# A selection matrix 192 instead of 64 bytes wide: everything allocated behind it starts 128 bytes later

## The chip, the cores and the metric

The kernel runs on one core of a Trainium2 chip. The metric is the device time of one execution in microseconds (us), median of several runs. TensorE does the matmuls (PE in the rows, its weight loads PEld), VectorE is DVE, ScalarE ACT, GpSimd POOL, and the queue of SyncE (SP) issues most DMAs. On-chip memory has 128 partitions; an address here is an offset in bytes within a partition, the same in all of them.

## What is computed

Three stages, one behind the other (cut to what matters):

```
# 1: attention with keys and values pooled by 8   (4 x 8 heads, 576 x 64)
attn = softmax(scale * q @ k_p.T);  x = attn @ v_p          # -> x: 2304 x 512
# 2: a dense layer
h = x @ w_in;  x = (h * np.cos(h)) @ w_out                  # 512 -> 2048 -> 512
# 3: eight experts, all applied, weighted by P
P = exp(x @ w_gate - max), then 8 rounds of row and column normalization
for e in range(8):
    h = np.maximum(x @ w1[e], 0.0)                          # 512 -> 1024
    out += P[:, e:e+1] * (h @ w2[e])                        # 1024 -> 512
```

## The kernel before

Every float32 product is made of three single-pass matmuls on pieces: each operand is cut into a high part and a low rest (xh and xl, whi and wlo, gh and gl, vhi and vlo), and hi·hi, hi·lo and lo·hi are added in PSUM.

The program is written as a graph of nodes, each for one engine (`Graph.add`, L169); `Graph.schedule` puts them in one fixed order per engine by estimated times and due times, and a table of numbers (`SHIFTS`) corrects some of them. None of these estimates reads an address.

Stage 2 works on blocks of 384 tokens. `hidden1` (L894 to L896) multiplies weights wc with xh and xl, `cosine` makes gh and gl, and `output1` (the same three lines, tile po) multiplies weights wc with gh and gl as the **moving** operand, 384 columns. For its last two blocks it uses seven products in place of eight (`first_layer`, L1077) with sums xP of the tokens and differences dhi and dlo of the weights; half of the resulting pieces lie in tiles named gw.

Stage 3 takes pairs of blocks (3) and half experts (16 units). In `first_layer` (L1077) the weights whi and wlo are the stationary operand and xc, the tokens' pieces, the moving one, 384 columns: 2 × 7 × 6 = 84 matmuls a step. Its results become the pieces gh and gl (`strassen_result`, `g_split`, `halves`). In `strassen_layer` (L1457) these are the **stationary** operand, in slices of 128 columns (512 bytes), and the weights vhi and vlo the moving one, 256 columns: 3 × 42 = 126 matmuls a step. The 48 steps follow each other, with blocks of the next step's first layer between those of the second layer (`STRASSEN`). `accumulate` (L1444) adds a result to the output.

```
for n, (l, m) in enumerate(((gh, w[name][0]), (gh, w[name][1]), (gl, w[name][0]))):
    nc.tensor.matmul(out=ps, lhsT=l[:, r], rhs=m[:, k], start=(start and h + n == 0),
```

Memory is a stack from the left and one from the right. From the left, in the order of allocation, come the group `base` (the x tiles, the first-layer weights, four accumulators, and then wgr, sel and lg of the gate), the group `first` (raw, gph and gpl: gh and gl), and `second`, which is later replaced by `more` (two more accumulators, further tiles for gh and gl). `sel` is a small matrix for picking columns; line L1206 reads its first 8 columns. From the right come the groups early, mid, ahead and late, with vhi and vlo, s, c and sf.

Where tiles start in the built program, in bytes past a multiple of 512:

| tiles | before | after |
|---|---|---|
| xc, xh and xl of blocks 0 to 3, xP, gw, spare; whi, wlo, wc in `base` | 192 | 192 |
| gh, gl; raw, wsum, xd; r; wc in `second`; xh and xl of blocks 4 and 5; two accumulators | 320 | 448 |
| vhi, vlo; dhi, dlo (some dhi, dlo: 448); sf, s, c | 128 | 128 |

Of the kernel before, what the change touches and what calls it, by code (L numbers as in the profile page):

```python
# [23 lines left out]
P = 128  # L24
T = B * S
DM = H * D
KC = DM // P
FU = 512
FC = FU // P
E = 8  # L30
# [3 lines left out]
NT = T // P  # L34
# [6 lines left out]
GW = 32  # L41
# [102 lines left out]
class Graph:  # L144
# [18 lines left out]
    def buf(self, kind, shape, dtype, name):  # L163
        return Buf(kind, shape, dtype, name)
# [268 lines left out]
def fused_kernel(ctx: ExitStack, tc: tile.TileContext, qT, kT, vT, v0, k1, v1, wa1, wb1, wa2, wb2, wg, out):  # L433
# [731 lines left out]
    for u in range(U1):  # L1165
# [16 lines left out]


    gate = {n: buf(k_gc[n], s, F32, n) for n, s in (
        ("ones", [P, P]), ("wgr", [P, KC, GW]), ("sel", [P, 2 * E]), ("lg", [P, NT, E]), ("pr", [P, NT, E]))}
    ones, wgr, sel, lg, pr = (gate[n] for n in ("ones", "wgr", "sel", "lg", "pr"))
    add("V", 0.17, lambda: nc.vector.memset(ones.tile, 1.0), [], [ones])
    load(lambda: wgr.tile, lambda: wg, P * KC * GW * 4, writes=[wgr])
# [397 lines left out]
```

## Time and profile before

| | |
|---|---|
| median of 3 runs | 1930.12 us (1927.75 to 1932.39) |
| the profiled execution | 1929.34 us, its span 1927.6 us |
| TensorE busy, matmuls / weight loads | 1907.3 / 1872.0 us, 13012 of each |
| VectorE, ScalarE, GpSimd busy | 1531.9, 1096.6, 427.4 us |
| mean granted TensorE clock | 0.999 of full speed |
| moved by DMA | 406.79 MB, 211 GB/s |

The span runs from the first to the last instruction; what lies around it is 1.7 us. A matmul's duration reaches from its start to the modelled end of its pipeline, so that successive matmuls overlap; the distance between two starts in the timeline says how fast they follow.

### The profile page before, as it was taken

The page shows a single profiled execution, that of the slowest core. Times are in us where ns is not written, and L with a number is a line of the kernel's source. Part 1 is how long each engine was busy: PE and PEld are TensorE (multiplying, and loading weights), DVE is VectorE, ACT ScalarE, POOL GpSimd, SP SyncE. Part 2 cuts the span into 40 slices and gives each one's busy share as a digit, 9 for nine tenths or more (in the row PEclk, how much of TensorE's full clock was granted, in tenths as well). Part 3 has the DMA queues.
Part 4 walks back from the last instruction along what each step waited for, and adds up shares of the span by engine and source line. Part 5 has one row for each costly group of instructions (what it writes and reads, how often), then busy time and mean ns, then how long its engine had stood idle before and what let it go on. Part 6 is the DMA issues. An engine that isn't in the chain of part 4 may idle for free.

```text
span 1927.6 us, 34292 instructions
## 1 busy us (share of the span) xinstructions
PE 1907.3 (99%) x13012; PEld 1872.0 (97%) x13012; DVE 1531.9 (79%) x2823; ACT 1096.6 (57%) x2354; POOL 427.4 (22%) x341
## 2 busy tenths in 40 slices
PE   8999999999999999999999999999999999999999
PEld 6789998899999999999999999999999999999998
DVE  8998888987787777777787787777777877877776
ACT  5664445675556666555556565565555565655553
POOL 2523245453202021212112021212121120212120
PEclk9999999999999999999999999999999999999999
DMA  8567564487656546546546455465465464554552
GB/s 294 169 193 236 194 198 138 176 288 239 231 225 229 228 186 237 212 181 236 211 177 262 168 231 229 184 238 210 183 236 211 178 262 170 229 231 180 229 216 113
DMA packets 107478, 406.79 MB, mean 211 GB/s; under 512 B 11825, under 2 KB 16561, under 8 KB 107313
## 3 DMA queue, kind: packets, MB, share of 16 engines
q1 hardware_dynamic: 106768, 403.55, 56.4%
q8 instruction: 102, 1.67, 0.4%
q0 software_dynamic: 544, 1.05, 0.3%
q14 instruction: 64, 0.52, 0.1%
HBM read 363.40 MB, written 41.16 MB: 210 GB/s over the span
## 4 chain that ended last, share of the span: by engine, by line
PE 91%; DVE 5%; ACT 1%; DMA 1%; issue 1%; POOL 0%; SPq 0%; DVEq 0%; POOLq 0%; ACTq 0%
PE pc L1457 21%; PE py L1077 17%; PE qc L1457 16%; PE pv L1077 11%; PE px L1077 11%; PE po L894 3%; PE po L895 3%; PE po L896 3%; PE ph L894 1%; PE ph L896 1%; PE ph L895 1%; PE ptr L803 0%; DVE at L540 0%; DVE cw L858 0%; PE psc L714 0%
## 5 line engine op out<-in xcount | busy, mean ns | idle before, releaser
L1457 PE MATMUL pc<-vhi,gl 128*128 128x256 f32 x1152 | 321.6, 279 | 0.0
L1457 PE MATMUL pc<-vhi,gh 128*128 128x256 f32 x1152 | 321.5, 279 | 0.0
L1457 PE MATMUL pc<-vlo,gh 128*128 128x256 f32 x1152 | 321.3, 279 | 0.0
L1077 PE MATMUL py<-xc,whi 128*128 128x384 f32 x1152 | 293.3, 335 | 0.0
L540 POOL TENSOR_TENSOR raw<-raw 128x512 f32<-128x512 f32 x45 | 59.1, 1314 | 895.4 <-DVE wlo L540 542.1
L540 DVE TENSOR_TENSOR gl<-sf,gh 128x384 fp32r<-128x384 f32 x384 | 228.4, 624 | 30.9 <-ACT gh L523 30.9
L523 ACT ACTIVATE gh<-sf 128x384 fp32r<-128x384 f32 x384 | 195.0, 524 | 92.1 <-DVE sf L540 90.1
L1457 PE MATMUL qc<-vhi,gh 128*128 128x256 f32 x864 | 243.6, 282 | 0.9 <-DVE qc L540 0.5
L1457 PE MATMUL qc<-vhi,gl 128*128 128x256 f32 x864 | 241.6, 280 | 0.0
L1457 PE MATMUL qc<-vlo,gh 128*128 128x256 f32 x864 | 240.8, 279 | 0.0
L1457 PEld LDWEIGHTS pc<-vlo,gh 128*128 128x128 f32 x1152 | 216.6, 188 | 0.0
L1457 PEld LDWEIGHTS pc<-vhi,gl 128*128 128x128 f32 x1152 | 216.3, 188 | 0.0
L1457 PEld LDWEIGHTS pc<-vhi,gh 128*128 128x128 f32 x1152 | 215.5, 187 | 0.1
L1077 PEld LDWEIGHTS py<-xc,whi 128*128 128x128 f32 x1152 | 199.7, 188 | 1.3 <-ACT py L523 0.6
L1077 PE MATMUL px<-xc,whi 128*128 128x384 f32 x768 | 195.8, 335 | 0.0
L1077 PE MATMUL pv<-xc,whi 128*128 128x384 f32 x768 | 195.8, 335 | 0.0
L1077 PE MATMUL py<-xc,wlo 128*128 128x384 f32 x576 | 193.2, 335 | 0.0
L1457 PEld LDWEIGHTS qc<-vhi,gh 128*128 128x128 f32 x864 | 161.8, 187 | 3.4 <-DVE qc L540 1.1
L1457 PEld LDWEIGHTS qc<-vlo,gh 128*128 128x128 f32 x864 | 162.5, 188 | 0.0
L1457 PEld LDWEIGHTS qc<-vhi,gl 128*128 128x128 f32 x864 | 162.3, 188 | 0.0
L1077 PEld LDWEIGHTS pv<-xc,whi 128*128 128x128 f32 x768 | 130.7, 188 | 0.0
L1077 PEld LDWEIGHTS px<-xc,whi 128*128 128x128 f32 x768 | 130.5, 188 | 0.0
(235 smaller groups left out, 4676.1 us busy)
## 6 DMA issues: line engine op xcount, KB each, us to landing
xc<-xc SPq DMA_DIRECT2D x357, 768.0 KB, 6.7
wc<-wac SPq DMA_DIRECT2D x112, 256.0 KB, 3.3
raw<-wa SPq DMA_DIRECT2D x48, 512.0 KB, 4.0
raw<-wb SPq DMA_DIRECT2D x48, 512.0 KB, 7.4
wac<-wc SPq DMA_DIRECT2D x64, 256.0 KB, 3.8
out<-acc SPq DMA_DIRECT2D x18, 256.0 KB, 2.0
qc<-qt SPq DMA_DIRECT2D x30, 128.0 KB, 3.1
wf<-cw SPq DMA_DIRECT2D x12, 256.0 KB, 3.6
```

What stands on the lines that cost most here:

```text
L523: lambda: nc.scalar.activation(out=out(), in_=in_(), func=func, **{k: v() if callable(v) else v for k, v in more.items()}),
L540: (nc.gpsimd if e == "G" else nc.vector).tensor_tensor(out=out(), in0=in0(), in1=in1(), op=op)
L894: nc.tensor.matmul(out=ps, lhsT=lh, rhs=rh, start=(i == 0), stop=False)
L895: nc.tensor.matmul(out=ps, lhsT=lh, rhs=rl, start=False, stop=False)
L896: nc.tensor.matmul(out=ps, lhsT=ll, rhs=rh, start=False, stop=(i == total - 1))
L1077: nc.tensor.matmul(out=ps(), lhsT=l[:, k], rhs=r[:, c, :], start=(start and c + n == 0), stop=(c + n == 3), skip_group_check=True)
L1457: nc.tensor.matmul(out=ps, lhsT=l[:, r], rhs=m[:, k], start=(start and h + n == 0), stop=(h + n == 3), skip_group_check=True)
```

## The change

The tile sel gets 48 columns of 4 bytes in place of 16. Only its first 8 are written and read, as before. The tiles behind it in the left stack start 128 bytes later; the instructions and their order are the same on all five engines.

```diff
     gate = {n: buf(k_gc[n], s, F32, n) for n, s in (
-        ("ones", [P, P]), ("wgr", [P, KC, GW]), ("sel", [P, 2 * E]), ("lg", [P, NT, E]), ("pr", [P, NT, E]))}
+        ("ones", [P, P]), ("wgr", [P, KC, GW]), ("sel", [P, 6 * E]), ("lg", [P, NT, E]), ("pr", [P, NT, E]))}
```

## Rows read from the trace of the kernel before

**Rows 1.** The page, part 1: busy us (share of the span) and instructions.
```profile
PE 1907.3 (99%) x13012; PEld 1872.0 (97%) x13012; DVE 1531.9 (79%) x2823; ACT 1096.6 (57%) x2354; POOL 427.4 (22%) x341
```
**Rows 2.** Chain of waits from 600 us to the end, shares by line.
```profile
by line: PE pc L1457 28.9%; PE qc L1457 21.8%; PE py L1077 21.0%; PE pv L1077 14.0%; PE px L1077 14.0%; DVE acc L1444 0.1%; issue 0.1%; DVE qc L540 0.0%
```
**Rows 3.** Windows view of 600 to 1900 us: busy us (instructions) by engine.
```profile
core 0: us, PE busy (x) PEld busy (x) DVE busy (x) ACT busy (x) POOL busy (x), PEclk, DMA share, GB/s
600.00:1900.00 1300.00, 1300.00 (x9272) 1298.31 (x9271) 1004.53 (x1832) 737.09 (x1634) 217.90 (x159) 1.00 0.55 212
```
**Rows 4.** The same window: of L1457 alone, of L1077 alone, and one group of each.
```profile
600.00:1900.00 1300.00, 719.80 (x5561) 704.39 (x5562) 1.00 0.55 212
...
600.00:1900.00 1300.00, 710.23 (x3711) 627.14 (x3709) 1.00 0.55 212
...
L1457 PE MATMUL pc<-vhi,gh 128*128 128x256 f32 x1060 | 295.7, 279 | 0.0
...
L1077 PE MATMUL py<-xc,whi 128*128 128x384 f32 x1060 | 269.6, 335 | 0.0
```
**Rows 5.** Timeline of TensorE around 1004 us: start us, us, what.
```profile
999.43 0.28 PE L1457 MATMUL pc<-vhi,gl 128*128 128x256 f32 x1
999.54 0.51 PE L1077 MATMUL px<-xc,whi 128*128 128x384 f32 x2
...
1004.34 0.28 PE L1457 MATMUL pc<-vhi,gl 128*128 128x256 f32 x1
1004.45 0.51 PE L1077 MATMUL pv<-xc,whi 128*128 128x384 f32 x2
...
1005.49 0.28 PE L1457 MATMUL qc<-vhi,gh 128*128 128x256 f32 x1
...
1008.20 0.28 PE L1457 MATMUL pc<-vhi,gl 128*128 128x256 f32 x1
1008.32 0.51 PE L1077 MATMUL py<-xc,whi 128*128 128x384 f32 x2
...
1009.36 0.28 PE L1457 MATMUL qc<-vhi,gh 128*128 128x256 f32 x1
```
**Rows 6.** Groups of TensorE, 100 to 600 us: count | busy us, mean ns | idle before.
```profile
L894 PE MATMUL po<-gh,wc 128*128 128x384 f32 x296 | 101.3, 342 | 1.1 <-DVE acc L533 0.7 <-DVE acc L540 0.4
L896 PE MATMUL po<-gh,wc 128*128 128x384 f32 x296 | 99.9, 337 | 0.0
L895 PE MATMUL po<-gl,wc 128*128 128x384 f32 x296 | 99.8, 337 | 0.0
...
L894 PE MATMUL po<-gw,wc 128*128 128x384 f32 x64 | 21.6, 338 | 0.0
L896 PE MATMUL po<-gw,wc 128*128 128x384 f32 x64 | 21.6, 337 | 0.0
L895 PE MATMUL po<-gw,wc 128*128 128x384 f32 x64 | 21.5, 336 | 0.0
...
L1077 PE MATMUL px<-xh,wc 128*128 128x384 f32 x64 | 19.0, 341 | 0.0
...
L1077 PE MATMUL py<-xP,dhi 128*128 128x384 f32 x64 | 16.4, 338 | 0.0
...
L1077 PE MATMUL py<-xP,wc 128*128 128x384 f32 x48 | 9.7, 336 | 0.0
...
L1077 PE MATMUL pv<-xP,dhi 128*128 128x384 f32 x32 | 8.3, 340 | 0.0
```
**Rows 7.** Groups of VectorE, 600 to 1900 us, columns as in rows 6.
```profile
L540 DVE TENSOR_TENSOR gl<-sf,gh 128x384 fp32r<-128x384 f32 x352 | 211.6, 631 | 28.1 <-ACT gh L523 28.1
...
L540 DVE TENSOR_TENSOR gl<-spare,gh 128x384 fp32r<-128x384 f32 x88 | 64.0, 727 | 5.7 <-ACT gh L523 5.7
...
L540 DVE TENSOR_TENSOR gl<-c,gh 128x384 fp32r<-128x384 f32 x88 | 53.1, 603 | 3.8 <-ACT gh L523 3.8
```
**Rows 8.** The page, part 6: DMA issues, count, KB each, us to landing.
```profile
raw<-wa SPq DMA_DIRECT2D x48, 512.0 KB, 4.0
raw<-wb SPq DMA_DIRECT2D x48, 512.0 KB, 7.4
```

## The prediction

> **What bounds the kernel now.** I read the page's busy shares first [rows 1]. TensorE is busy for 1907.3 of 1927.6 us and its weight loads for 1872.0 us; VectorE has 79% and ScalarE 57%. The chain of waits for the last part of the run, from 600 us on, says the same more sharply [rows 2]: 28.9 + 21.8% of it is the second layer's matmul line L1457, 21.0 + 14.0 + 14.0% the first layer's line L1077, and only some tenths of a per cent anything else. In the window 600 to 1900 us TensorE has 1300.00 of 1300.00 us, at a granted clock of 1.00, the upper of its two levels, while VectorE has 1004.53 and ScalarE 737.09 us [rows 3]. So in this part the time is a count of matmuls times the step from one matmul's start to the next.
>
> The program issues the same instructions in the same order on all five engines before and after; only addresses differ. What can change is therefore a duration or a step, and the step is the thing to read. A matmul's own duration (279 or 335 ns [rows 4]) overlaps its successor's and is no step. The timeline gives steps [rows 5]: the second layer's 24 matmuls from 1005.49 to 1008.32 us take 2.83 us, so 117.9 ns each; the first layer's six from 1008.32 to 1009.36 take 1.04 us, so 173.3 ns each. The counts agree: the window has 5,561 second-layer and 3,711 first-layer matmuls [rows 4], and 5,561 × 0.1179 + 3,711 × 0.1733 = 1,299 us of the 1,300.
>
> Over the whole program the second layer has 16 units × 3 pairs × 3 row tiles × 42 = 6,048 matmuls, that is 713 us, 37% of the run. **One nanosecond on this step is worth 6.05 us, or 0.31%.** A measurement of this kernel can tell about 0.2% (3.9 us) from no change, which is 0.64 ns on this step.
>
> **The change part by part.** It widens the tile sel from 64 to 192 bytes per partition. Nothing reads the added bytes. All that stands behind sel in the left stack moves by 128 bytes, and nothing else moves.
>
> *Second layer, the main term.* Its stationary operand is a 512-byte piece of gh or gl, which moves from 320 to 448 past a multiple of 512; its moving operand, vhi or vlo, stays at 128. So each weight load, which runs during the matmul before it, reads at 192 bytes past the moving stream (modulo 512) before and at 320 after, which is 192 bytes the other way. No row shows a second layer with another distance, so I bound the cost from both sides. Below: at the first layer's rate per column (173.3/384 × 256 = 115.5 ns [rows 5]) a step would be 2.4 ns shorter, −14.5 us; in the first layer both operands stand at 192, so its distance is 0. Above: in the first phase the same moving tile xP takes 336 ns with the weights wc and 338 ns with dhi, which lies elsewhere [rows 6]; 2 ns on each of 6,048 steps is +12.1 us. The rest of that view is as tame: the means of the 384-column groups lie between 336 and 342 ns, whichever of 128, 192, 320 and 448 their operands start at. I take 0, because the distance stays the same in size and only turns its sign, and because the row nearest to zero cost, wc against dhi, is in itself as near to nothing as the view resolves. The two ends stay for the range.
>
> The Trainium skill (SBUF — State Buffer, "Who interferes with whom") gives TensorE two read ports, one for the moving operand and one for weight loads, and says that TensorE and ScalarE never wait on anyone. By that rule the main term is 0 whatever the addresses. No row here separates the two ports, so I keep the bounds.
>
> *First phase.* The first dense layer's second product has gh and gl as its moving operand, 296 × 3 = 888 matmuls whose start moves from 320 to 448. The same line has a control: in 64 × 3 of them the moving tile is gw, which stands at 192 and stays. The means are 342, 337, 337 ns against 338, 337, 336 [rows 6], so the position costs 1.7 ns at most: −1.5 us if 448 is as good as 192, +1.5 us if it is as much worse again; I take −0.4 us. The x tiles of the last two blocks (line L1077, px<-xh,wc and its neighbours, some 160 matmuls) show 341 against 336 ns for xP: 160 × 5 ns is ±1 us at most, and I take 0. The weights that share the moved region are a part of wc and show in the same rows.
>
> *VectorE and ScalarE.* They write and read gh and gl, 352 of the largest group in the window at 631 ns, and 88 each at 727 and 603 ns with other sources [rows 7]. Should these change by a tenth, 528 × 63 ns = 33 us are added to 1004.5 of 1300 us: the idle 295 us of VectorE hide it, and the chain gives VectorE about 0.1% [rows 2]. If that cover went, TensorE would wait for gl at the head of the second layer; nothing in the chain shows that it is near. I cost it at 0.
>
> *Transfers.* raw moves by 128 bytes too: 96 loads of 512 KB that land 4.0 and 7.4 us after issue [rows 8], unit by unit and ahead of use. The packets stay as they are and the DMA share is 0.55 [rows 3]: 0.
>
> *Sum.* 0 − 0.4 + 0 + 0 = −0.4 us on the profiled execution's 1929.34 us gives 1928.9; the median of the runs shown, 1930.12, is 0.8 us higher. I predict **1929 us**.
>
> **The rivals.**
>
> *The new distance is a better one, so the run is faster.* For it: the second layer's step is 117.9 ns where the first layer's rate per column would make it 115.5, so there is something to lose. The last matmul ahead of a first-layer block loads weights that stand at 192, 64 bytes off its moving operand; it starts its successor after 0.11 us in two of the three cases shown, where 0.12 is the commoner step [rows 5]. Against it: that is the last digit of the view, and it may only be a matter of where a start is recorded. At 115.5 ns the time is 1929 − 14.5 = 1914.5 us; half of it gives 1922. It shows from 0.64 ns on.
>
> The Trainium skill (TensorE: Matmul & The Clock Gate, "Back-to-back issue gap") puts a warm matmul at N/2.4 + 2.5 ns, an estimate of 109 ns for 256 columns; by that the second layer would have 8.7 ns, 53 us, to lose. The first layer's 173.3 ns against the 162.5 of that formula says that the trace doesn't reach it at distance 0 either.
>
> *The new distance is a worse one, so the run is slower.* Place: each second-layer weight load against the moving stream. Price: up to the 2 ns above, which gives 1941 us; half of it 1935. It decides from 0.64 ns on, because TensorE has no idle time to hide it in. For it: 37% of the run hangs on one operand pair, which has one fixed distance, so that any loss repeats 6,048 times. Against it: in the first phase tiles that start at 448 (a part of dhi) are in groups of 338 to 340 ns, no worse than those at 320 with 337 to 342 [rows 6].
>
> *The change doesn't move what it names.* Pools could round a tile to a larger size. In the built program lg, raw, gh, gl and the rest do start 128 bytes later, and whi, vhi and xc don't, so I give this no chance of its own.
>
> **How the numbers follow.** No change, 0.40: 1929, its own range 1926 to 1934. Faster by a better distance, 0.34: 1914.5 to 1926. Slower by a worse one, 0.26: 1934 to 1941. The faster side has the larger share, because the step has 2.4 ns that another layer of the same run does without, and because the first phase's spread favours leaving 320 rather than staying. The range runs from 1911 to 1943: the two bounds, with 2 to 3.5 us at each end for the first phase and for the runs' own spread. Some 2 in 10 are left out, since the bounds come from other shapes.
>
> **What the changed profile would show.** If I am right, a run of 24 second-layer matmuls still takes 2.82 to 2.84 us in the timeline, and six of the first layer 1.04. The faster case shows 2.77 to 2.81 for the 24, the slower one 2.85 to 2.88, with the first layer unchanged. L894 to L896 with gh and gl would stand at 337 to 342 ns. The forecast's reasons would be wrong if the time moved while these steps stayed: then TensorE waits, and the chain of waits must name VectorE or a transfer with more than the tenths of a per cent that it has now.

## The result, and the profile after

The changed kernel takes 1905.69 us (median of four runs, 1904.52 to 1909.63), the kernel before, run beside it, 1929.34 (1927.75 to 1932.39). The ratio is 0.9879, with a 95% interval of 0.9859 to 0.9899: **23.65 us faster**, where 1929 us and no change were predicted, with a range that ended at 1911. The profiled execution took 1906.59 us, its span 1904.9; that is 22.75 us less than the one before.

The page, part 1, of the changed kernel, to be held against [rows 1]:

```profile
PE 1883.8 (99%) x13012; PEld 1846.4 (97%) x13012; DVE 1528.8 (80%) x2823; ACT 1095.2 (57%) x2354; POOL 431.0 (23%) x341
```

TensorE has lost 23.5 us of busy time with the same 13,012 matmuls; the others are within 4 us of what they had. The chain of waits from 600 us to the end, as in [rows 2]:

```profile
by line: PE pc L1457 28.4%; PE qc L1457 21.6%; PE py L1077 21.4%; PE pv L1077 14.2%; PE px L1077 14.2%; DVE acc L1444 0.1%; issue 0.1%; DVE qc L540 0.0%
```

The second layer's line L1457 has gone from 50.7 to 50.0% of the chain, and nothing but matmuls has a share. The windows view of 600 to 1900 us, all, then L1457 alone, then L1077 alone (columns as in [rows 3, 4]), and one group of L1457:

```profile
600.00:1900.00 1300.00, 1299.50 (x9433) 1296.35 (x9432) 1018.22 (x1863) 743.74 (x1653) 221.77 (x159) 1.00 0.55 213
```
```profile
600.00:1900.00 1300.00, 715.83 (x5707) 701.55 (x5708) 1.00 0.55 213
```
```profile
600.00:1900.00 1300.00, 713.55 (x3726) 630.14 (x3724) 1.00 0.55 213
```
```profile
L1457 PE MATMUL pc<-vhi,gl 128*128 128x256 f32 x1088 | 300.3, 276 | 0.0
```

The same 1300 us now hold 9,433 matmuls in place of 9,272, at the same granted clock of 1.00, and TensorE is idle for only 0.5 us of them. The 276 ns of the group are a mean duration, 279 before [rows 4], and no step. The step itself stands in the timeline of TensorE around 993 us (start us, us, what), to be read as [rows 5] were:

```profile
993.10 0.33 PE L1077 MATMUL py<-xc,wlo 128*128 128x384 f32 x1
993.27 0.28 PE L1457 MATMUL qc<-vhi,gh 128*128 128x256 f32 x1
993.39 0.28 PE L1457 MATMUL qc<-vlo,gh 128*128 128x256 f32 x1
...
995.88 0.28 PE L1457 MATMUL pc<-vhi,gl 128*128 128x256 f32 x1
995.99 0.52 PE L1077 MATMUL pv<-xc,whi 128*128 128x384 f32 x2
```

The 24 second-layer matmuls from 993.27 to 995.99 us take 2.72 us, 113.3 ns each; before it was 2.83 us and 117.9 ns.

For the sum I added up, over the whole trace, the distance from each matmul's start to the next one's start, by line. "Sum of steps" below is always this; it is worked out from the trace and is no row of it. L1457 fell from 713.5 to 690.9 us, **−22.6**; L1077 rose by 1.1; the first phase's lines L894 to L896 fell by 2.1 together; no other line moved by more than 0.8. Of the second layer's matmuls, 5,566 are followed by another one without a longer wait: 655.0 to 631.4 us, −23.6, or 117.7 to 113.4 ns each. The 427 that are followed by a first-layer matmul gave 0.4 us (they were at 114.4 ns and are at 113.5). The 54 steps of more than 125 ns, where a block's head waits, cost 1.3 us more than before.

So the time came from one place, the step of the second layer, and nearly the whole of it arrived at the end.

### The profile page after: what moved, and what is told of

Its sections match the earlier page's. It is cut to its first block, busy times and chain, and to the rows that moved or that the text cites. A ratio compares the mean times of both kernels' runs of the same rounds, so it can differ in the third digit from the quotient of the medians.

```text
span 1904.9 us, 34292 instructions
## 1 busy us (share of the span) xinstructions
PE 1883.8 (99%) x13012; PEld 1846.4 (97%) x13012; DVE 1528.8 (80%) x2823; ACT 1095.2 (57%) x2354; POOL 431.0 (23%) x341
## 4 chain that ended last, share of the span: by engine, by line
PE 92%; DVE 5%; ACT 1%; DMA 1%; issue 1%; SPq 0%; DVEq 0%; ACTq 0%
PE pc L1457 20%; PE py L1077 17%; PE qc L1457 16%; PE px L1077 11%; PE pv L1077 11%; PE po L894 3%; PE po L896 3%; PE po L895 3%; PE ph L894 2%; PE ph L896 2%; PE ph L895 2%; PE ptr L803 0%; DVE at L540 0%; PE psc L714 0%; DVE m L854 0%
## 5 line engine op out<-in xcount | busy, mean ns | idle before, releaser
L1457 PE MATMUL pc<-vlo,gh 128*128 128x256 f32 x1152 | 318.0, 276 | 0.0
L1457 PE MATMUL pc<-vhi,gl 128*128 128x256 f32 x1152 | 318.0, 276 | 0.0
L1457 PE MATMUL pc<-vhi,gh 128*128 128x256 f32 x1152 | 318.0, 276 | 0.0
L1077 PE MATMUL py<-xc,whi 128*128 128x384 f32 x1152 | 293.7, 335 | 0.0
L1457 PE MATMUL qc<-vhi,gh 128*128 128x256 f32 x864 | 241.6, 280 | 1.0 <-DVE qc L540 0.5
L1457 PE MATMUL qc<-vlo,gh 128*128 128x256 f32 x864 | 238.8, 276 | 0.0
L1457 PE MATMUL qc<-vhi,gl 128*128 128x256 f32 x864 | 238.8, 276 | 0.0
L1457 PEld LDWEIGHTS pc<-vhi,gh 128*128 128x128 f32 x1152 | 216.3, 188 | 0.1
L1457 PEld LDWEIGHTS pc<-vhi,gl 128*128 128x128 f32 x1152 | 216.3, 188 | 0.0
L1457 PEld LDWEIGHTS pc<-vlo,gh 128*128 128x128 f32 x1152 | 216.2, 188 | 0.0
L1077 PEld LDWEIGHTS py<-xc,whi 128*128 128x128 f32 x1152 | 199.3, 188 | 1.3 <-ACT py L523 0.6
L1077 PE MATMUL px<-xc,whi 128*128 128x384 f32 x768 | 196.1, 336 | 0.0
L1077 PE MATMUL pv<-xc,whi 128*128 128x384 f32 x768 | 196.1, 336 | 0.0
L1077 PE MATMUL py<-xc,wlo 128*128 128x384 f32 x576 | 192.5, 334 | 0.0
L1457 PEld LDWEIGHTS qc<-vhi,gh 128*128 128x128 f32 x864 | 162.2, 188 | 4.8 <-DVE qc L540 1.1
L1457 PEld LDWEIGHTS qc<-vhi,gl 128*128 128x128 f32 x864 | 162.3, 188 | 0.0
L1457 PEld LDWEIGHTS qc<-vlo,gh 128*128 128x128 f32 x864 | 162.1, 188 | 0.0
L1077 PEld LDWEIGHTS pv<-xc,whi 128*128 128x128 f32 x768 | 130.3, 188 | 0.0
L1077 PEld LDWEIGHTS px<-xc,whi 128*128 128x128 f32 x768 | 130.1, 188 | 0.0
```

The lines of the kernel that those rows point to most:

```text
L1077: nc.tensor.matmul(out=ps(), lhsT=l[:, k], rhs=r[:, c, :], start=(start and c + n == 0), stop=(c + n == 3), skip_group_check=True)
```

## The experiments

An address here is a start past a multiple of 512 bytes. The **distance** is the stationary operand's start (gh, gl) minus the moving operand's (vhi, vlo), modulo 512: 192 before, 320 after. Each kernel is the kernel before with the edit shown (f4 is the changed kernel with its edit); of the line with sel only the changed entry stands in the edits. On each engine all of them issue the same instructions in the same order; only addresses differ, in f4 also a width. `edge` is an unused tile at the right end of a group; widening it for the group mid moves vhi and vlo down. Where memory runs short, `dynamic_dma_scratch_size` goes from 2048 to 1536 (in g2 to 1024); e2 has that edit as well and shows that it is worth nothing.

Theory **A**: the distance decides. Rivals: the place of gh and gl alone decides, or other tiles that moved do.

**e1: the change's distance, made from the other side.** gh stays at 320, vhi goes to 0.

```diff
-            edge.tile([P, 8], F32, name="edge" + self.name)
+            edge.tile([P, 40 if self.name == "mid" else 8], F32, name="edge" + self.name)
```

> gh and gl stay at 320; vhi and vlo go from 128 to 0 (a wider edge tile on the right), so the weight load starts 320 bytes past the moving stream, as in the changed kernel. Theory A (the distance of the two operands, modulo 512, sets the second layer's step): step 113 to 114 ns, time 1903 to 1909 us. Theory B (the place of gh, gl and their neighbours sets it: 320 is slow, 448 fast): step 117 to 118 ns, time 1926 to 1932 us.

**e2: both moved by 128, the distance as before.** gh at 448 as in the changed kernel, vhi at 256.

```diff
-            edge.tile([P, 8], F32, name="edge" + self.name)
+            edge.tile([P, 104 if self.name == "mid" else 8], F32, name="edge" + self.name)
...
-("sel", [P, 2 * E])
+("sel", [P, 48])
...
-dynamic_dma_scratch_size=2048
+dynamic_dma_scratch_size=1536
```

> gh and gl at 448 as in the changed kernel, but vhi and vlo at 256 too, so that the distance is 192 bytes as before (the scratch for software DMA descriptors is 512 bytes smaller to make room). Theory A: step 117 to 118 ns, time 1926 to 1932 us. Theory B: step 113 to 114 ns, 1903 to 1909 us.

e1 took 1912.4 us, ratio 0.9911 (0.9893 to 0.9929); e2 1928.74, ratio 0.9999 (0.999 to 1.0009). The same group in both, from the groups by line of TensorE, 600 to 1900 us: count | busy us, mean ns | idle before.

```profile
L1457 PE MATMUL pc<-vhi,gl 128*128 128x256 f32 x1082 | 299.0, 276 | 0.0
```
```profile
L1457 PE MATMUL pc<-vhi,gl 128*128 128x256 f32 x1057 | 295.9, 280 | 0.0
```

e1 gains without a byte of sel, and e2 has everything the changed kernel moved and gains nothing. So far what decides is where the two operands of the second layer stand to each other, and neither the place of gh and gl nor that of other tiles (f1 and g1 to g4 will show that it isn't the whole). e2 is as theory A expected. e1's time is 3 us above A's range, because e1 gets 71% of the gain: its sum of steps is 697.0 us, since a block of it (second-layer matmuls that follow each other with no other matmul between) starts with steps of 117, 122, 116 and 114 ns before it settles at 113.

**e3 and e4: two distances between and beyond.** 256 and 384.

```diff
-("sel", [P, 2 * E])
+("sel", [P, 32])
```

> sel 128 bytes wide: gh and gl at 384, vhi at 128, distance 256. Theory A1 (distance modulo 256; 64 and 320 alike fast, 192 slow): this is like distance 0, of which the second layer shows nothing; by the first layer, which has distance 0 and its usual step, neither slow nor fast by much: 113 to 118 ns, 1905 to 1930 us. Theory A2 (the load must run well behind or ahead of the stream, more distance the better up to 320): a step between 118 and 113.5 ns, near 115.5, time near 1917 us. Theory B: between the two places, no number.

```diff
-("sel", [P, 2 * E])
+("sel", [P, 64])
```

> sel 256 bytes wide: gh and gl at 0, vhi at 128, distance 384. Theory A1 (modulo 256, like 128, which in the first phase of the kernel before went with steps of 175 to 176 ns where 173 to 174 was usual): slow, 117 ns or more, 1926 us or more. Theory A2 (from 192 to 320 better and better): 113 ns or less, 1900 to 1906 us.

Both are slower than before: 1937.41 us, ratio 1.0043 (1.0026 to 1.0059), and 1936.46, 1.0042 (1.0029 to 1.0056). So 320 is an island and not the start of a good stretch, and it is no matter of a distance of zero modulo 256. Of e3's expectations, both theories with a number for the time (1905 to 1930, near 1917) missed; e4 came out as A1 expected, and against A2.

**e5 to e8: round the circle.** 448, 0, 64 and 128, with the widths 80, 96, 112 and 128 for sel; e7 and e8 with the smaller scratch.

```diff
-("sel", [P, 2 * E])
+("sel", [P, 80])
```

> sel 320 bytes wide: gh and gl at 64, vhi at 128, distance 448. So far the step is 117.7 ns at distance 192, 119.6 at 256, 113.4 at 320, 118.6 at 384. Theory A1 (the pattern repeats after 256 bytes): 448 is like 192, 117 to 118 ns, 1926 to 1932 us. Theory A3 (it repeats after 512 bytes only, with one fast place near 320): no number is fixed, some 115 to 120 ns, 1915 to 1940 us; a step at 114 or less would speak against both.

```diff
-("sel", [P, 2 * E])
+("sel", [P, 96])
```

> sel 384 bytes wide: gh and gl at 128, vhi at 128, distance 0. Theory A1: like 256, 119 to 120 ns, 1934 to 1940 us. Theory A3: open, 115 to 120 ns. A third theory C (the load must not start on the same place as the stream, every other distance differs by details): worst of all here, over 120 ns and 1940 us.

```diff
-("sel", [P, 2 * E])
+("sel", [P, 112])
...
-dynamic_dma_scratch_size=2048
+dynamic_dma_scratch_size=1536
```

> sel 448 bytes wide and the software DMA's scratch 512 bytes smaller: gh and gl at 192, vhi at 128, distance 64. Theory A1: like 320, 113 to 114 ns, 1903 to 1910 us; for it also speaks that the last second-layer matmul ahead of a first-layer block, which loads weights 64 bytes off, had a step of 114.3 ns in the kernel before. Theory A3: 117 to 120 ns, 1926 to 1940 us.

```diff
-("sel", [P, 2 * E])
+("sel", [P, 128])
...
-dynamic_dma_scratch_size=2048
+dynamic_dma_scratch_size=1536
```

> sel 512 bytes wide and the scratch 512 bytes smaller: gh and gl at 256, vhi at 128, distance 128. Theory A1: like 384, 118 to 119 ns, 1930 to 1937 us. Theory A3: open; in the first phase of the kernel before, matmuls with this distance had steps of 175 to 176 ns where 173 to 174 was usual, which would make it one of the slow ones.

All kernels in which only the tiles behind sel move, gh and gl among them, in the order of the distance:

| distance (modulo 256) | kernel | us | ratio to before, 95% | step, ns | sum of steps, us |
|---|---|---|---|---|---|
| 0 (0) | e6 | 1936.73 | 1.0036 (1.0023 to 1.0049) | 119.6 | 723.5 |
| 256 (0) | e3 | 1937.41 | 1.0043 (1.0026 to 1.0059) | 119.6 | 723.5 |
| **64 (64)** | e7 | 1905.33 | 0.987 (0.9855 to 0.9885) | 113.4 | 690.9 |
| **320 (64)** | after | 1905.69 | 0.9879 (0.9859 to 0.9899) | 113.4 | 690.9 |
| 128 (128) | e8 | 1939.29 | 1.0043 (1.003 to 1.0056) | 118.9 | 720.1 |
| 384 (128) | e4 | 1936.46 | 1.0042 (1.0029 to 1.0056) | 118.9 | 720.0 |
| 192 (192) | before | 1929.34 | 1 | 117.7 | 713.5 |
| 448 (192) | e5 | 1928.1 | 0.9993 (0.9983 to 1.0002) | 117.7 | 713.5 |

The column step is a mean over the inside of the blocks, without the first and last steps of a block. In the traces, distances of 64 and 192 have one steady step inside a block. At 0 the steps settle at 120 ns after the first three; at 128 they never settle but repeat 117, 122, 120, 119 and 115 ns, so that 118.9 is a mean of unlike steps.

One group stands for each; the row is the same as above, of e3, e4, e5, e6, e7 and e8:

```profile
L1457 PE MATMUL pc<-vhi,gl 128*128 128x256 f32 x1054 | 297.5, 282 | 0.0
```
```profile
L1457 PE MATMUL pc<-vhi,gl 128*128 128x256 f32 x1055 | 295.8, 280 | 0.0
```
```profile
L1457 PE MATMUL pc<-vhi,gl 128*128 128x256 f32 x1060 | 295.9, 279 | 0.0
```
```profile
L1457 PE MATMUL pc<-vhi,gl 128*128 128x256 f32 x1054 | 297.5, 282 | 0.0
```
```profile
L1457 PE MATMUL pc<-vhi,gl 128*128 128x256 f32 x1088 | 300.3, 276 | 0.0
```
```profile
L1457 PE MATMUL pc<-vhi,gl 128*128 128x256 f32 x1052 | 294.9, 280 | 0.0
```

The pairs agree to 0.1 us in 700: **the pattern repeats after 256 bytes**. e7 and the changed kernel even share their row, 1,088 matmuls at 276 ns. The two placements that look most alike by size, 192 and 320 (64 short of 256, and 64 past it), are 4.3 ns apart. The steps are those of theory A1 in all four runs, and so are the times, but for e8, whose median lies 2 us above A1's range (its ratio, 1.0043, is next to e4's); theory C's worst case at 0 did not come.

**f2 and f3: between the multiples of 64.** 352 and 288, which are 96 and 32 modulo 256.

```diff
-("sel", [P, 2 * E])
+("sel", [P, 56])
```

> sel 224 bytes wide: gh and gl at 480, vhi at 128, distance 352, which is 96 modulo 256. If the step changes smoothly with the distance, it lies between 113.4 ns (64) and 118.9 (128): 115 to 117 ns, 1914 to 1928 us. If there is a flat fast stretch around 64: 113 to 114 ns, 1904 to 1908 us. If starts off a multiple of 64 cost by themselves: above 119 ns, over 1938 us.

```diff
-("sel", [P, 2 * E])
+("sel", [P, 40])
```

> sel 160 bytes wide: gh and gl at 416, vhi at 128, distance 288, which is 32 modulo 256. Smooth: between 119.7 ns (0) and 113.4 (64), so 115 to 118 ns, 1914 to 1931 us. Flat fast stretch around 64: 113 to 114 ns, 1904 to 1908 us. A cost of starts off a multiple of 64: above 119 ns, over 1938 us.

1935.65 us, ratio 1.0042 (1.0029 to 1.0056), and 1938.5, 1.0059 (1.0044 to 1.0074). Their second-layer steps alternate between 116 and 122 ns, sums 720.0 and 717.6 us; in f3 the first layer's line grew as well, to 768.5 us. Both the smooth change and the flat fast stretch missed. The cost of starts off a multiple of 64 has f3's time in its range, but the steps of both kernels average under its 119 ns, so that no expectation held. Of the distances tried, only 64 modulo 256 is good, with a loss 32 bytes to either side of it.

**f1: the distance of the changed kernel, with the first layer moved.** A pad of 64 bytes ahead of the pool of whi and wlo puts them at 256 against xc's 192, so that the first layer's own distance is 64; gh is kept at 448 and vhi at 128. (In f1, f4, g3 and g4 the second layer's line is L1460, since lines were added ahead of it.)

```diff
+            if pool == "wp":
+                pad = self.stack.enter_context(self.graph.tc.tile_pool(name="pad", bufs=1, side=self.side))
+                pad.tile([P, 16], F32, name="pad")
...
-("sel", [P, 2 * E])
+("sel", [P, 32])
```

> A pad of 64 bytes ahead of the first layer's weights (whi, wlo at 256, xc at 192: distance 64) and sel 128 bytes wide, so that gh and gl are at 448 and the second layer's distance is 320 as in the changed kernel. Theory D (the first layer too pays for its distance, which was 0): its step falls below 173.3 ns; if by as much as the second layer's from 0 to 64 (6 ns), 4,032 x 6 = 24 us less than the changed kernel, near 1881 us. Theory E (with 384 columns the load has room beside the stream and the distance doesn't set the step): 173 to 174 ns, 1904 to 1908 us.

1929.89 us, ratio 1.0012 (1.0003 to 1.0021): the whole gain is gone, though the second layer's operands stand exactly as in the changed kernel. Its group, and its timeline around 1000 us:

```profile
L1460 PE MATMUL pc<-vhi,gl 128*128 128x256 f32 x1059 | 298.6, 282 | 0.0
```
```profile
1000.45 0.28 PE L1460 MATMUL qc<-vhi,gh 128*128 128x256 f32 x1
...
1003.16 0.28 PE L1460 MATMUL pc<-vhi,gl 128*128 128x256 f32 x1
1003.28 0.51 PE L1080 MATMUL pv<-xc,whi 128*128 128x384 f32 x2
```

24 matmuls in 2.83 us again, 117.9 ns. In the last block of the program no first-layer matmul comes in between, and 125 steps follow each other at 117.7 ns, until TensorE waits for VectorE; the four behind that wait are 122, 116, 114 and 113 ns. Six blocks early in stage 3 begin behind a matmul of the gate and not of the first layer: in f1 all six settle at 113.3 ns, in the changed kernel five of the same six at 117.7. The first layer did not get faster at distance 64 either: its step is 173.3 ns as at 0. So theory D missed, and theory E was right on the first layer's step and wrong on the time (1904 to 1908). Theory A falls in its plain form. What takes its place, theory **M**: at 64 modulo 256 the step *can* be 113.4, and how a block begins selects it.

**f4: a wider moving operand, to tell the loads from the stream.** The changed kernel, in which the products P1 and P2 of one sort read 272 columns in place of 256.

```diff
+            wide, ps = (True, ps) if ps.shape[-1] > HD else (False, ps)
...
+                if wide:
+                    k = slice(h * 192, h * 192 + HD + 16)
...
+            P0 = lambda p=p: p[:, :HD + 16]
...
-            pe(mm(12, HD), two_products(p0, "P1", p1, "P5", True), needs("P1", "P5"), [p], goal=goals[i][0])
+            pe(mm(12, HD), two_products(P0, "P1", p1, "P5", True), needs("P1", "P5"), [p], goal=goals[i][0])
```

> The changed kernel with the moving operand of products P1 and P2 of the second layer 272 columns wide in place of 256 (16 columns of other products' sums are added to, and half of the columns are read from elsewhere in the tile, so this part of the output is another sum); the distance stays 64 modulo 256. Theory L (at the fast distance the weight load sets the step): the step of these matmuls rises by 3 ns or less over 113.4. Theory S (the stream of columns sets it): by 16 columns at the first layer's 0.45 ns each, 7 ns.

1935.6 us, from one execution. The question stays open: the wide steps take 122 to 126 ns, about 10 more than 113.4, which is above what either answer asked for; counted from 117.7 it would be about 6 (12 of them in 1.48 us are 123.3 ns each), near the second answer, but which step to count from is what this kernel doesn't tell. Its use is another one. The timeline of TensorE from 1000 us on:

```profile
1000.87 0.28 PE L1460 MATMUL pc<-vhi,gl 128*128 128x272 f32 x1
1001.00 0.28 PE L1460 MATMUL pc<-vhi,gh 128*128 128x256 f32 x1
...
1001.70 0.51 PE L1077 MATMUL px<-xc,whi 128*128 128x384 f32 x2
...
1011.41 0.34 PE L1077 MATMUL py<-xc,wlo 128*128 128x384 f32 x1
1011.59 0.28 PE L1460 MATMUL qc<-vhi,gh 128*128 128x256 f32 x1
...
1013.63 0.52 PE L1077 MATMUL px<-xc,whi 128*128 128x384 f32 x2
```

Six 256-column matmuls behind wide ones take 0.70 us, 117 ns each; eighteen that begin a block take 2.04 us, 113.3 each. That is one kernel with both steps at one distance, divided by what ran ahead.

**g1 to g4: where M should show.** g1 moves gh and vhi together by 64 from the changed kernel's pair, the first layer left alone. g2 puts them at 256 and 192, a distance of 64. g3 moves the pair as g1 and the first layer as f1. g4 keeps the changed kernel's pair with the first layer at distance 192.

```diff
-            edge.tile([P, 8], F32, name="edge" + self.name)
+            edge.tile([P, 24 if self.name == "mid" else 8], F32, name="edge" + self.name)
...
-("sel", [P, 2 * E])
+("sel", [P, 32])
```

> First layer at distance 0 (both at 192); gh and gl at 384, vhi and vlo at 64, distance 320. Theory F (the second layer's distance and the first layer's fix the step): 113.4 ns, 1903 to 1909 us. Theory M (at distance 64 modulo 256 there are two steady steps, 113.4 and 117.7 ns; how a block begins selects one, and that hangs on where gh stands against xc too, here 192 bytes instead of 256 or 0): either of the two and nothing steady between, so 1903 to 1913 or 1926 to 1932 us.

```diff
-            edge.tile([P, 8], F32, name="edge" + self.name)
+            edge.tile([P, 120 if self.name == "mid" else 8], F32, name="edge" + self.name)
...
-("sel", [P, 2 * E])
+("sel", [P, 128])
...
-dynamic_dma_scratch_size=2048
+dynamic_dma_scratch_size=1024
```

> First layer at distance 0 (both at 192); gh and gl at 256, vhi and vlo at 192, distance 64 (the scratch for software DMA 1024 bytes smaller). Theory F: 113.4 ns, 1903 to 1909 us. Theory M: 113.4 or 117.7 ns; the blocks begin with gh 64 bytes past xc.

```diff
-            edge.tile([P, 8], F32, name="edge" + self.name)
+            edge.tile([P, 24 if self.name == "mid" else 8], F32, name="edge" + self.name)
...
+                pad.tile([P, 16], F32, name="pad")
```

> First layer at distance 64 (whi, wlo at 256, xc at 192) as in the slow f1; gh and gl at 384, vhi and vlo at 64, distance 320. Theory F: 117.7 ns as in f1, since both layers' distances are f1's, 1926 to 1932 us. Theory M: it can be fast here, 113.4 ns after the first matmuls of a block, because gh now stands 192 bytes past xc: then 1900 to 1913 us.

```diff
+                pad.tile([P, 48], F32, name="pad")
...
-("sel", [P, 2 * E])
+("sel", [P, 128])
...
-dynamic_dma_scratch_size=2048
+dynamic_dma_scratch_size=1536
```

> First layer at distance 192 (whi, wlo at 384, xc at 192); gh and gl at 448, vhi and vlo at 128 as in the changed kernel, distance 320 (the scratch 512 bytes smaller). Theory F: open, only that the second layer's step is the same in all blocks. Theory M: 113.4 or 117.7 ns. First layer: if its distance sets its step at all, not 173.3 ns here.

| kernel | gh / vhi, first layer's distance | us | ratio to before, 95% | steady steps, ns | sum of steps, us |
|---|---|---|---|---|---|
| after | 448 / 128, 0 | 1905.69 | 0.9879 | 113.4 | 690.9 |
| f1 | 448 / 128, 64 | 1929.89 | 1.0012 (1.0003 to 1.0021) | 117.6 | 716.6 |
| g4 | 448 / 128, 192 | 1928.53 | 0.9999 (0.9989 to 1.0008) | 117.7 | 713.7 |
| e1 | 320 / 0, 0 | 1912.4 | 0.9911 (0.9893 to 0.9929) | 113 behind each head | 697.0 |
| g1 | 384 / 64, 0 | 1927.76 | 0.9991 (0.9978 to 1.0003) | both | 705.0 |
| g3 | 384 / 64, 64 | 1924.79 | 0.9973 (0.996 to 0.9986) | both | 705.9 |
| g2 | 256 / 192, 0 | 1929.43 | 1.0008 (0.9998 to 1.0017) | 117.7 | 715.3 |

All seven have the distance 64 modulo 256. g1 shows both steps side by side in one timeline:

```profile
971.47 0.34 PE L1077 MATMUL py<-xc,wlo 128*128 128x384 f32 x1
971.64 0.28 PE L1457 MATMUL pc<-vhi,gh 128*128 128x256 f32 x1
...
974.35 0.28 PE L1457 MATMUL pc<-vhi,gl 128*128 128x256 f32 x1
974.47 0.51 PE L1077 MATMUL pv<-xc,whi 128*128 128x384 f32 x2
```
```profile
1004.94 0.34 PE L1077 MATMUL pv<-xc,wlo 128*128 128x384 f32 x1
1005.12 0.28 PE L1457 MATMUL qc<-vhi,gh 128*128 128x256 f32 x1
...
1007.73 0.28 PE L1457 MATMUL pc<-vhi,gl 128*128 128x256 f32 x1
1007.85 0.51 PE L1077 MATMUL py<-xc,whi 128*128 128x384 f32 x2
```

24 matmuls in 2.83 us, and 33 us later 24 in 2.73, with operands at the same starts past a multiple of 512. Of its blocks of 12 matmuls and more that have no longer wait in them, all 136 that follow two first-layer products (six matmuls each) step at 117.7, and 173 of the 175 that follow one at 113.3. g1 still gains nothing, because its first-layer blocks have steps of 170 to 185 ns and their sum rises by 8 us to 770.3. In g3 the timeline shows two neighbouring blocks:

```profile
1003.47 0.28 PE L1460 MATMUL qc<-vhi,gh 128*128 128x256 f32 x1
...
1006.18 0.28 PE L1460 MATMUL pc<-vhi,gl 128*128 128x256 f32 x1
1006.30 0.51 PE L1080 MATMUL pv<-xc,whi 128*128 128x384 f32 x2
...
1007.35 0.28 PE L1460 MATMUL qc<-vhi,gh 128*128 128x256 f32 x1
...
1009.95 0.28 PE L1460 MATMUL pc<-vhi,gl 128*128 128x256 f32 x1
1010.07 0.51 PE L1080 MATMUL py<-xc,whi 128*128 128x384 f32 x2
```

117.9 and 113.3 ns. But here the number of products ahead does not divide them: after two, 85 blocks step at 117.7 and 51 at 113.3; after one, 86 and 89. What does divide them, inside one kernel, is the step that leads into the block, from the last first-layer matmul's start to the first second-layer one's (0.17 and 0.18 us in the lines of g1). In g1 it is 179 or 180 ns ahead of all 173 blocks at 113.3 ns and 173 to 176 ahead of all 140 at 117.7. In g3 it is 173 or 174 ns ahead of 133 of the 140 blocks at 113.3, and 169 to 171, 175 or 176 ahead of 171 of the 173 at 117.7. So how two neighbouring matmuls stand in time at the head goes with the step that follows; that it causes the choice is not shown, and no one value holds for all kernels (173 ns leads into blocks at 117.7 in g1 and into blocks at 113.3 in the changed kernel).

Theory F, that the distances of both layers fix one step, is out: g2 has the changed kernel's two distances modulo 256 and steps at 117.7, and g1 and g3 have both steps in one kernel. That both occur, with nothing steady between, is what M says, so M holds in that; but its range for g2 and g4 allowed either step, which makes those two no test of it, and g3's time missed M's 1900 to 1913. In g4 the first layer's commonest step is 173 ns at distance 192 as well, so its distance sets no step there that these runs can see. What in the beginning selects the step (these kernels show a hand in it for the products ahead, for their distance and for the place of the pair) isn't settled.

## Why the prediction was wrong

**What bounds the kernel: right.** TensorE was all but never idle, the step was the thing to read, and 1 ns on it is worth 6.05 us: 4.3 ns on the inner 5,566 steps is all of the gain. The expectation for a wrong forecast was stated, too: the time moved *with* the step, and no wait took a share of the chain.

**The main term failed, at one sentence:** "I take 0, because the distance stays the same in size and only turns its sign." That is true modulo 512, and it took for granted that the size counts and the sign doesn't. The runs show a period of 256 in which 192 and 448 are one case, 64 and 320 another; 64 before the moving operand is a 117.7 ns step, 64 behind it can be 113.4. So the term that was put at 0 measured −22.6 us. The second reason, that dhi costs next to nothing against wc, compared mean durations of 384-column matmuls. The same text says that a duration is no step; in the second layer 3 ns less of duration went with 4.3 ns less of step.

**The lower bound was too near.** It took the first layer's rate per column as the best that a step could be (115.5 ns, −14.5 us). The second layer reaches 113.4 [rows 5 give 117.9]; per column that is 0.443 ns against the first layer's 0.451. The two layers share no rate, since a first-layer step stays at 173.3 ns at distance 0 as well as 64 (f1), while the second layer at the first layer's distance of 0 is at its slowest (119.6 ns, e3 and e6). The end of the range fell with it: −22.6 us lay 8 beyond the bound, and the 2.72 us for 24 matmuls lie below the 2.77 to 2.81 that the text gave for the faster case.

**The rival that came true** had the mechanism and the place, a better distance in the second layer; its price of 14.5 us should have been 22.6, and the time lies outside the 1914.5 to 1926 that it was given. One of its two reasons was the first layer's rate, which doesn't hold. The other, the last step ahead of a first-layer block, was real: 114.4 ns on average over the 427 such steps of the trace, where the inner ones had 117.7. I set that aside as the last digit of a view. But the reading of it, weights 64 bytes off their moving operand, doesn't hold by itself either: in e3, e4, e6, e8, f2 and f3 these two operands stand exactly as before, and the step is 117.0 to 118.2 ns; in e1 they stand 192 apart, and it is 113.6. As far as these runs show, the hint pointed the right way by luck.

**The rule on the ports.** The step at one shape, one clock and one order of instructions lies between 113.4 and 119.6 ns by position alone. The Trainium skill (SBUF — State Buffer, "Who interferes with whom") says that TensorE never waits on anyone, and by that the main term is 0. The trace doesn't agree, if the difference arises in the reads of memory, which no run here shows.

The Trainium skill (TensorE: Matmul & The Clock Gate, "Back-to-back issue gap") gives the formula that the prediction took, an estimate of 109 ns for 256 columns, for an isolated matmul. For a stream with a weight load ahead of each matmul, as this kernel has, it states about 81 ns at 128 columns and about 131 at 512. The trace agrees with neither: the best step here is 113.4 ns at 256 columns, and 384 columns take 173.3, more than it states for 512.

**First phase: −0.4 predicted, −2.1 measured.** The control failed. I held gh's 342, 337, 337 ns against gw's 338, 337, 336 [rows 6] as the cost of the position. After the change the same groups are:

```profile
L894 PE MATMUL po<-gh,wc 128*128 128x384 f32 x296 | 100.6, 340 | 1.1 <-DVE acc L533 0.6 <-DVE acc L540 0.5
L896 PE MATMUL po<-gh,wc 128*128 128x384 f32 x296 | 99.2, 335 | 0.4 <-DMA wc<-wac 0.4
L895 PE MATMUL po<-gl,wc 128*128 128x384 f32 x296 | 99.0, 334 | 0.0
L894 PE MATMUL po<-gw,wc 128*128 128x384 f32 x64 | 21.5, 336 | 0.0
L896 PE MATMUL po<-gw,wc 128*128 128x384 f32 x64 | 21.5, 335 | 0.0
L895 PE MATMUL po<-gw,wc 128*128 128x384 f32 x64 | 21.4, 334 | 0.0
```

gw, which did not move, fell by 2 ns as well. A part of the weights wc stands behind sel and moved, so gw was no clean control. Two of the other runs bear on the period here: e7 (gh at 192) has 339, 335, 334 ns in the first three groups, as after, while e5 (64) has the 342, 337, 337 of before. (e1 and e2 repeat before and after, since gh and wc stand there as in those.) Against the wc of `base`, at 192, the faster kernels have a distance of 0 modulo 256 and the slower ones 128. In e3 it is 64, and the groups have 341, 337, 337 ns: the distance that is good in the second layer is not the good one here.

**VectorE and transfers: 0, as predicted.** The group of [rows 7], over the whole run:

```profile
L540 DVE TENSOR_TENSOR gl<-sf,gh 128x384 fp32r<-128x384 f32 x384 | 227.6, 622 | 30.2 <-ACT gh L523 30.1
```

raw lands 4.4 and 7.8 us after issue, where [rows 8] have 4.0 and 7.4, and has no share in the chain. The cover got thinner, though: VectorE has 1018 us of the same 1300, and the 54 long steps of the second layer cost 1.3 us more.

**The slower rival** didn't come true at this distance, but it was real: e3, e4, e6, e8, f2 and f3, six placements of the same tiles, stand at 1935 to 1939 us, in its range.

## What to carry to other kernels

Where TensorE is never idle, measure the step from start to start of each shape of matmul, and ask where its two operands start to each other: the distance was worth 1.2% in a kernel in which no wait was left. A good distance is no recipe: f1, g2 and g4 have the second layer's distance of the changed kernel, modulo 256, and none of its gain, so each layout has to be timed. Bound such a term by the spread over *distances*, tried in one sweep of padding, and not by another layer's rate, and treat a sign as a case of its own. A control counts only when both of its operands stayed where they were.

## What the runs showed of the hardware

- With one weight load (128 × 128) per matmul of 256 columns at a granted clock of 1.00, the step depends on where the stationary slice starts against the moving one. With the moving tiles and the first layer left in their places it repeats after 256 bytes: 119.6 ns at 0, 113.4 at 64, a mean of 118.9 at 128, 117.7 at 192, and 116 to 122 by turns at 32 and 96.
- At 64 modulo 256 there are two steady steps, 113.4 and 117.7 ns. A block keeps the one it settles at in its first matmuls, for 125 steps in f1. Moving tiles that the second layer doesn't read (the first layer's weights, with the accumulators behind them) can switch it, which cost 24 us in f1 and 23 in g4.
- At 64 modulo 256 the step that leads into a block goes with the one it keeps: in g1, 179 or 180 ns ahead of 113.3, 173 to 176 ahead of 117.7.
- Why the distance acts, and what at a block's head selects the step, was not found. Nor is it shown that 113 ns belongs to 64 alone: in the kernel before, at 192, the last four steps, behind a wait of TensorE, are 114, 113, 113 and 114 ns, too few to say what they would have settled at. f4 was meant to separate the weight loads from the moving stream and did not. Nothing shows that 113.4 is the least that can be had; of the sixteen kernels that were tried none beat the changed one, and e7 equals it (1905.33 us).
